# Order of plain and dilated heads, and the place of the rank matmuls, in a fused attention and expert kernel

## The chip, the cores and the metric

The kernel runs on one core of a Trainium2 chip. Its time is the device time of one execution in microseconds (us), as the median of several runs. The profile is of one further execution, with the hardware profiler on. Engines are named as in its page: PE is TensorE's matmuls, PEld its weight loads, DVE is VectorE, ACT is ScalarE, POOL is GpSimd and SP is SyncE; a "q" behind a name is the engine's sequencer, which also issues DMAs.

## The reference

Attention over 8 sequences of 576 tokens with 8 heads of 64, then one expert layer over the 4608 tokens (model width 512, 8 experts, hidden width 1024), each token going to one expert. Everything is float32.

```python
rel = pos[:, None] - pos[None, :]
mask_plain = (rel >= 0) & (rel < 32)                       # heads 0 to 3
mask_dil = (rel >= 0) & (rel < 32 * 4) & (rel % 4 == 0)    # heads 4 to 7
attn = softmax(where(mask, q @ k.T / 8, -1e9))
x = (attn @ v).transpose(0, 2, 1, 3).reshape(4608, 512)
logits = x @ w_gate
expert = argmax(logits, 1); gate = softmax(logits)[expert]
out = gate * (maximum(x @ w1[expert], 0) @ w2[expert])
```

## The kernel before

**Attention.** A head sees only a band, so scores are computed in blocks of 64 queries by 96 keys, nine blocks a head. For dilated heads the tokens are first put in order of their remainder by 4, which makes four strips of 144 tokens in which the mask is the same band. A *unit* is two heads of one kind in one sequence: `units` (line 472) lists `(b, ty, hl)`, 32 in all, with `ty` 0 for plain and 1 for dilated heads, and before the change plain comes first. Of a unit, `turn` transposes q and k on TensorE (lines 323 and 330) and copies them out of PSUM (VectorE for q, line 314, ScalarE for k, line 316). `front` makes the scores (line 366) and their row minima on VectorE (line 382); for sequences 0 to 3 (`EARLY`) the mask is added by matmuls (line 354), for later ones on VectorE. `exponentials` runs on ScalarE (line 403), `norm` on VectorE and GpSimd (lines 415 to 418), `weights` transposes the result (line 428) and VectorE copies it out (`eT`, line 430), `summed` multiplies by v (line 443). A unit's weights are made two units behind its scores (`LAG`), its sums three behind.

**Loads.** `load_qk` and `load_v` issue the DMAs from SyncE's queue; only k of sequence 0 goes by ScalarE's queue. A plain q or k of a sequence is 4 DMAs, one a head, in runs of 256 bytes (line 262). A dilated one is 4 DMAs, one for each of the four pieces of its strips, all four heads together, in runs of 512 bytes (line 269). v is 5 DMAs for plain heads and 13 for dilated ones. Each of these tiles has one buffer, so the load for the next sequence waits until the engines have read the last one, and SyncE's queue is in order. The mask tiles come by GpSimd's queue (`load_masks`): the first holds `turn` and `even0`, for plain heads, the second `even1` and `odd1`, for dilated ones.

**Routing.** `row_part` transposes the attention's output into token rows and `logit_part` makes the gate's logits (line 560), adding up over the four units of a sequence. When the last unit of a sequence has given its logits, `route(b)` starts: transpose of the logits (`lg`, line 577), one-hot vectors of the best expert and running counts on VectorE (lines 597 to 618, `before` being the counts), then two matmuls into `rank` (lines 625 and 632) that give each token its place in its expert, then the places as integers and six indirect DMAs from GpSimd that scatter the rows into a `bucket` in HBM (line 234). `tables` then works out, in small VectorE instructions, which expert's rows each *slot* of 128 tokens takes.

**Expert layer.** `moe` goes through some 37 slots. Of a slot, x is fetched from the bucket (line 1075), transposed (line 1150), multiplied by w1 (line 1218), then by w2 (line 1250), scaled and scattered to the output (line 1267). Weights are fetched by SyncE (line 1094).

**What sets the order.** The whole kernel is written as three generators that yield pieces: attention, routing and slots. A loop at the end takes one piece of attention (five a unit), then enough pieces of slots to keep a planned rate, and then one piece of routing. `yield` in `route` is thus what puts distance between two steps of routing. A finished table lets its slots start `BEHIND` = 12 planner's us later. After the last piece of attention, each piece of routing is given 2 us of slots:

```python
    while routing:
        clock["owed"] = 2.0
        run_slots()
        run_routing()
```

Within this, the scheduler of the language places instructions in each engine's in-order queue. All matmul outputs but the logits share one pool of seven PSUM banks (`bank`). `tc.issue_after(i)` makes what is issued in it stand behind instruction i on its engine.

Of the kernel before, what the change touches and what calls it, by code (L numbers as in the profile page):

```python
# [79 lines left out]
def _constants():  # L80


    def band(j, ty):

        qi, ki = 64 * j + np.arange(64)[:, None], max(0, 64 * j - WIN) + np.arange(96)[None]
        seen = (qi - ki >= 0) & (qi - ki < WIN)
        if ty:
            seen &= qi // STRIP == ki // STRIP
        return np.where(seen, 0.0, BIG)

    def mask(ty):

        pairs = [(0, 1), (2, 3), (4, 5), (6, 7), (8, 8)]
        return np.concatenate([np.concatenate([band(j, ty) for j in two]) for two in pairs], 1)

    p = np.arange(128)
    e = np.arange(E)

    parts = {"add0": mask(0)[:, 0:384], "add1": mask(1)}
    for name, ty, js in (
        ("even0", 0, (0, 2, 4, 6, 8, 8)), ("even1", 1, (0, 2, 4, 6, 8)), ("odd1", 1, (1, 3, 5, 7, 8))
    ):
        parts[name] = np.tile(np.concatenate([band(j, ty) for j in js], 1), (2, 1))
    parts["turn"] = np.tile(np.eye(64), (2, 1))

    exact, mask_at = [], {}
    for names in (("turn", "even0"), ("even1", "odd1"), ("add0", "add1")):
        n = 0  # L110
        for name in names:
            mask_at[name] = len(exact), n
            n += parts[name].shape[1]
        some = np.concatenate([parts[name] for name in names], 1).astype(np.float32)
        exact.append(np.ascontiguousarray(some.astype(ml_dtypes.bfloat16)))
    mask_at["odd0"] = mask_at["even0"][0], mask_at["even0"][1] + 96
    parts = {
        "tri": np.triu(np.ones((128, 128)), 1)[:, :96],
        "ones": np.ones((128, 128)),
        "rev": np.tile(E - e, (128, 1)),  # L120
        "ecap": np.tile(e * CAP, (128, 1)),
        "tok": p[:, None] + TT * np.arange(NT)[None],
        "row": p[:, None],
        "eidx": np.tile(np.minimum(np.arange(E1), E - 1), (128, 1)),
        "twice": np.tile(2 * np.arange(NSLOT), (128, 1)),
    }
    parts["first"] = np.tile(np.append(np.arange(E)[::-1] / E, -1e6), (128, 1))


    for s, (_, j0, j1) in enumerate(STAGES[:-1]):  # L130
        k = np.arange(j1 - j0)
        n = (j1 - j0 + 1) // 2
        parts[f"list{s}"] = np.tile(k // 2 + n * (k % 2), (128, 1))


    k, i, m = np.arange(NSLOT - J0), np.arange(NMIX), np.arange(NMIX + 1)
    n = k[:, None] - (np.array(MIX)[None] < k[:, None]).astype(int) @ (i[:, None] < m[None])
    last = {}
    last["plan"] = np.concatenate([n // 2, n % 2]).reshape(1, -1)
    last["many"] = m  # L140
    last["i2"] = i
    last["ends"] = -1 - i
    own = [[G * (g if g < n else g - n) for g in range(4)] for n in KIND]
    last["own"] = (np.array(own).reshape(1, -1))
    last["later"] = (G * np.array(KIND))
    at, k, cols = {}, 0, []
    for name, a in parts.items():
        full = np.zeros((128, a.shape[1]), np.float32)
        full[: a.shape[0]] = a
        at[name] = (k, a.shape[1])  # L150
        k += a.shape[1]
        cols.append(full)
    last_at, k = {}, 0
    for name, a in last.items():
        last_at[name] = (k, a.size)
        k += a.size
    last = np.concatenate([a.reshape(1, -1) for a in last.values()], 1).astype(np.float32)
    return np.ascontiguousarray(np.concatenate(cols, 1)), at, exact, mask_at, np.ascontiguousarray(last), last_at
# [3 lines left out]
def kernel(  # L162
# [46 lines left out]
    def const(name, rows=128):  # L209
        a, w = at[name]  # L210
        return cst[0:rows, a : a + w]
# [40 lines left out]

    t = {}

    def load_qk(b, ty):
        for name, src, queue in (("q", q, nc.sync), ("k", k, nc.sync if b else nc.scalar)):
            if ty == 0:
                x = pool.tile([TT, NT, 4, DH], F32, tag=name + "0", name=f"{name}0_{b}", bufs=1)  # L260
                for h in range(4):
                    queue.dma_start(x[:, :, h, :], src[b, h].rearrange("(t p) d -> p t d", p=TT))
            else:


                x = pool.tile([96, 4, 3, 128], F32, tag=name + "1", name=f"{name}1_{b}", bufs=1)
                a = src[b, 4:8].rearrange("h (t m a) d -> m t h (a d)", m=2, a=2)
                for i, p0, m, t0, n in ((0, 0, 0, 0, 96), (1, 0, 0, 96, 48), (1, 48, 1, 0, 48), (2, 0, 1, 48, 96)):
                    queue.dma_start(x[p0 : p0 + n, :, i], a[m, t0 : t0 + n])
            t[b, name, ty] = x  # L270

    def first_key(j):
# [32 lines left out]
    def turn(b, ty, hl, name):  # L305

        src = t[b, name, ty]

        def copy(out, in_):

            if name == "q":
                nc.vector.tensor_scalar(out, in_, -SCALE, None, op0=OP.mult)  # L314
            else:
                nc.scalar.copy(out, in_)  # L316

        dst = pool.tile([128, S], F32, tag=name + "T", name=name + "T", bufs=2)
        for a in range(2):
            ps = bank("turned")  # L320
            if ty == 0:
                for i in range(3):
                    nc.tensor.transpose(  # L323
                        ps[:, TT * i : TT * i + TT],
                        src[:, 3 * a + i, 2 * hl : 2 * hl + 2, :].rearrange("p h d -> p (h d)"),
                        ident[0:TT, 0:TT],
                    )
            else:
                for i in range(3):
                    nc.tensor.transpose(  # L330
                        ps[:, 96 * i : 96 * i + 96], src[:, 2 * hl + a, i], ident[0:96, 0:96]
                    )
            copy(dst[:, 288 * a : 288 * a + 288], ps[:, 0:288])
        return dst
# [134 lines left out]
    def attention():  # L469


        units = [(b, ty, hl) for b in range(B) for ty in range(2) for hl in range(2)]
        load_masks(0)
        for ty in range(2):
            load_qk(0, ty)
        load_masks(1)
        for ty in range(2):
            load_v(0, ty)

        wrote_bucket(nc.sync.dma_start(bucket[E * CAP : NROWS], blank), 0)  # L480
        qT = {n: turn(0, 0, 0, n) for n in "qk"}
        evs, dens, eTs, xTs = {}, {}, {}, {}
        for i in range(len(units) + LAG + 3):

# [23 lines left out]
            if 0 <= u - 1 < len(units):  # L508
                b2, ty2, hl2 = units[u - 1]
                logit_part(b2, 2 * ty2 + hl2, xTs.pop(u - 1))  # L510
                ended = b2 if (ty2, hl2) == (1, 1) else None
            yield 3.0, ended

            if 0 <= i - LAG < len(units):
# [19 lines left out]

    def row_part(b, c, xT):

        if c == 0:
            rows[b] = pool.tile([TT, NT, ROW], F32, tag="rows", name=f"rows_{b}")
            logits[b] = lpsum.tile([96, 2 * TT], F32, tag="logits", name=f"logits_{b}")
            nc.gpsimd.tensor_scalar(  # L540
                rows[b][:, :, DM + 1], const("tok", TT), float(b * S), None, op0=OP.add
            )
        for i in range(0, NT, 3):
            ps = bank("xrow")
            for n in range(3):
                nc.tensor.transpose(
                    ps[0:TT, 128 * n : 128 * n + 128],
                    xT[:, TT * (i + n) : TT * (i + n) + TT],
                    ident,
                )  # L550
            (nc.scalar.copy, nc.vector.tensor_copy)[i // 3](
                rows[b][:, i : i + 3, 128 * c : 128 * c + 128],
                ps[0:TT, 0:384].rearrange("p (t d) -> p t d", t=3),
            )

    def logit_part(b, c, xT):


        for j in range(3):
# [1 line left out]
                logits[b][32 * j : 32 * j + 32],  # L561
                lhsT=wg[:, c],
                rhs=xT[:, 2 * TT * j : 2 * TT * j + 2 * TT],
                start=c == 0,
                stop=c == 3,
            )

    def route(b):
# [47 lines left out]
        for i in range(NT):  # L616
# [1 line left out]
            nc.vector.tensor_tensor(  # L618
                out=before[:, n + 1], in0=before[:, n], in1=oh[:, i], op=OP.add
            )  # L620
        yield
        yield
        ps = bank("rank")
        rk = ps[0:TT, 0 : NT * E]
        nc.tensor.matmul(
            rk,
            lhsT=const("tri", TT),
            rhs=oh.rearrange("p t e -> p (t e)"),
            start=True,
            stop=False,  # L630
        )
        nc.tensor.matmul(
            rk,
            lhsT=const("ones", TT)[:, 0:TT],
# [27 lines left out]
    def tables(s):  # L662
# [5 lines left out]
        scratch = None  # L668
        if last:

            scratch = pool.tile([96, 4, 9, DH], F32, tag="v0", name="scratch", bufs=1)
            scratch = scratch.rearrange("p a b c -> p (a b c)")[0:1]
            width = packed_last.shape[1]
            nc.scalar.dma_start(
# [698 lines left out]
```

## Time and profile before

| | |
|---|---|
| time, median of 3 runs | 785.97 us (782.84 to 792.31) |
| time of the profiled execution | 786.18 us |
| its span in the profile | 784.4 us |
| granted TensorE clock, mean | 0.981 |
| PE busy | 744.8 us, 95% of the span |
| DVE, ACT, POOL busy | 279.7, 226.2, 146.2 us |
| DMA | 195.41 MB, 249 GB/s in the mean |
| first scores (L366) | 12.57 us |
| first slot's transposes (L1150) | 121.43 us |
| last tables of routing done | 524.7 us |
| last slot's w2 matmuls (L1250) begin | 764.60 us |

The span falls into a start until about 36 us, in which the first loads arrive, attention alone until 121 us, attention and slots together until the middle of the span, and slots alone after that. Starts and durations are in us from the span's start. In a timeline the number in brackets is how long the engine stood idle before, and what ended that. In a list of waits the numbers are the total, how often, and the longest. In windows, each engine has its busy time and its instructions, followed by the granted clock, the DMA engines' busy share and GB/s.

### The profile page before, as it was taken

What the parts mean: (1) busy time and instruction counts of PE and PEld (TensorE: products, weight loads), DVE (VectorE), ACT (ScalarE), POOL (GpSimd) and SP (SyncE); (2) the same over time, 40 slices, a digit from 0 to 9 for tenths busy, and PEclk for the clock granted to TensorE, in tenths of its full rate; (3) what the DMA queues carried; (4) which work ended last, traced back from release to release, by engine and by line L of the source; (5) the groups of instructions that cost most, each with busy time, mean ns of one, the idle gap of its engine ahead of it and who ended that gap; (6) DMA issues with size and microseconds to landing.
All of it is one profiled execution on the core that took longest, in us unless ns stands there. A gap on an engine that the chain in (4) does not pass through costs nothing. (4 is left out here: it accounts for less than half of the span.)

```text
span 784.4 us, 17928 instructions
## 1 busy us (share of the span) xinstructions
PE 744.8 (95%) x6774; PEld 555.8 (71%) x6774; DVE 279.7 (36%) x954; ACT 226.2 (29%) x853; POOL 146.2 (19%) x142
## 2 busy tenths in 40 slices
PE   5798898989999899999999999999999999999993
PEld 4686788778777677777777776786776383686781
DVE  3577779646334333353333421271010111111010
ACT  3696685533532233333322110100100100100100
POOL 0424334214112311122011300160000000000000
PEclk9899889999999999999999999999999999999997
DMA  9777589998998997999217827999980583983995
GB/s 202 191 146 207 143 214 302 298 255 254 314 300 274 353 321 225 313 333 342 74 53 246 285 94 279 320 340 390 330 302 32 201 307 133 327 288 130 325 316 206
DMA packets 179612, 195.41 MB, mean 249 GB/s; under 512 B 73552, under 2 KB 105952, under 8 KB 179522
## 3 DMA queue, kind: packets, MB, share of 16 engines
q1 hardware_dynamic: 166896, 169.01, 69.8%
q0 software_dynamic: 6928, 20.53, 7.4%
q10 hardware_dynamic: 5698, 4.67, 2.1%
q8 instruction: 57, 0.93, 0.5%
q14 instruction: 33, 0.27, 0.1%
HBM read 216.14 MB, written 21.54 MB: 303 GB/s over the span
## 5 line engine op out<-in xcount | busy, mean ns | idle before, releaser
L1218 PEld LDWEIGHTS ph<-xt,w 128*128 128x128 f32 x2240 | 259.9, 192 | 19.7 <-issue 16.9
L1218 PE MATMUL ph<-xt,w 128*128 128x128 f32 x2240 | 268.7, 276 | 3.1 <-DMA w<-in_moe_w_dram 2.1
L1250 PE MATMUL py<-w,h 128*128 128x512 f32 x560 | 255.2, 596 | 0.0
L1250 PEld LDWEIGHTS py<-w,h 128*128 128x128 f32 x560 | 100.2, 190 | 98.4 <-issue 96.0
L1267 POOL DMA_INDIRECT out_dram<-y,to x35 | 34.6, 988 | 322.6 <-ACT y L1261 306.1
L1152 DVE COPY xt<-xt 128x512 f32<-128x512 f32 x38 | 26.2, 690 | 184.7 <-PE xt L1150 184.5
L1261 ACT ACTIVATE y<-py,x 128x512 f32<-128x512 f32 x35 | 24.0, 687 | 217.2 <-PE py L1250 166.7
L418 POOL TENSOR_TENSOR e<-e,rec 128x864 f32<-128x864 f32 x32 | 52.2, 1631 | 173.1 <-DVE rec L417 104.3
L430 DVE COPY eT<-weights 96x384 f32<-96x384 f32 x96 | 47.7, 545 | 31.5 <-PE weights L428 31.2
L234 POOL DMA_INDIRECT bucket<-rows,idx x48 | 44.5, 927 | 72.4 <-DVE idx L651 60.2
L403 ACT ACTIVATE e<-e,lo 128x96 f32<-128x96 f32 x144 | 51.8, 361 | 13.7 <-DVE lo L395 13.7
L403 ACT ACTIVATE e<-scores,lo 128x96 f32<-128x96 f32 (+1 forms) x160 | 52.7, 345 | 4.5 <-DVE lo L382 4.1
L1238 DVE TENSOR_SCALAR h<-ph 128x512 f32<-128x512 f32 x35 | 24.1, 689 | 73.4 <-PE ph L1218 73.3
L1229 ACT ACTIVATE h<-ph 128x512 f32<-128x512 f32 x35 | 20.9, 597 | 86.3 <-PE ph L1218 82.4
L443 PEld LDWEIGHTS xo<-eT,v 96*64 96x64 f32 x1216 | 40.6, 145 | 6.4 <-issue 2.0
L443 PE MATMUL xo<-eT,v 96*64 96x64 f32 (+1 forms) x1216 | 44.9, 231 | 0.2 <-ACT kT L316 0.2
L316 ACT COPY kT<-turned 128x288 f32<-128x288 f32 x64 | 22.6, 406 | 58.7 <-PE turned L330 34.9
L428 PE MATMUL weights<-ident,e 128*96 128x128 f32 x288 | 38.8, 282 | 0.8 <-POOL e L418 0.8
L428 PEld LDWEIGHTS weights<-ident,e 128*96 128x96 f32 x288 | 32.8, 131 | 9.0 <-issue 7.6
L366 PE MATMUL scores<-kT,qT 64*64 64x96 f32 x1152 | 37.0, 258 | 0.0
L366 PEld LDWEIGHTS scores<-kT,qT 64*64 64x64 f32 x1152 | 31.7, 141 | 6.7 <-issue 3.8
L314 DVE TENSOR_SCALAR qT<-turned 128x288 f32<-128x288 f32 x64 | 26.3, 447 | 28.0 <-PE turned L323 16.1
(213 smaller groups left out, 589.2 us busy)
## 6 DMA issues: line engine op xcount, KB each, us to landing
w<-in_moe_w_dram SPq DMA_DIRECT2D x164, 1024.0 KB
x<-bucket SPq DMA_DIRECT2D x26, 257.0 KB
v<-in_v_dram SPq DMA_DIRECT2D x32, 192.0 KB
q<-in_q_dram SPq DMA_DIRECT2D x32, 144.0 KB
v<-in_v_dram SPq DMA_DIRECT2D x48, 96.0 KB
k<-in_k_dram SPq DMA_DIRECT2D x28, 144.0 KB
q<-in_q_dram SPq DMA_DIRECT2D x16, 192.0 KB
x<-bucket ACTq DMA_DIRECT2D x11, 257.0 KB
```

The source lines that it names most:

```text
L234: nc.gpsimd.indirect_dma_start(out=bucket, out_offset=bass.IndirectOffsetOnAxis(ap=idx, axis=0), in_=rows, in_offset=None, bounds_check=NR ...
L314: nc.vector.tensor_scalar(out, in_, -SCALE, None, op0=OP.mult)
L366: nc.tensor.matmul(sc[r][64 * c : 64 * c + 64, 96 * (i % 5) : 96 * (i % 5) + 96], lhsT=qT[rows, 64 * j : 64 * j + 64], rhs=kT[rows, first_ ...
L403: nc.scalar.activation(out=e[p0:p1, i], in_=s[:, 96 * (i - i0) : 96 * (i - i0) + 96], func=AF.Exp, bias=lo[p0:p1, i : i + 1], scale=-1.0, ...
L418: return nc.gpsimd.tensor_tensor(out=e, in0=e, in1=rec.unsqueeze(2).broadcast_to([128, 9, 96]), op=OP.mult)
L428: nc.tensor.transpose(tp[0:96, 128 * i : 128 * i + 128], e[:, a + i], ident)
L430: nc.vector.tensor_copy(eT, tp[0:96, 0:384])
L443: nc.tensor.matmul(xo[DH * h : DH * h + DH, at0 : at0 + nq], lhsT=vt[:, 2 * hl + r, j, :] if ty == 0 else vt[:, hl, j, DH * r : DH * r + D ...
L1152: nc.vector.tensor_copy(xt, ps)
L1218: nc.tensor.matmul(ph[:, fi], lhsT=w1[:, c, 128 * f : 128 * f + 128], rhs=xt[:, c], start=c == 0, stop=c == 3,)
L1250: nc.tensor.matmul(py, lhsT=h[:, f], rhs=w2[:, f], start=f == 0, stop=f == 7)
L1267: i = nc.gpsimd.indirect_dma_start(out=out, out_offset=bass.IndirectOffsetOnAxis(ap=to, axis=0), in_=y, in_offset=None, bounds_check=N - 1 ...
```

## The change

Units run dilated heads first in each sequence, and everything that names the first or last unit of a sequence follows (the start and end of the logits' sum, when the row tile is made, when a sequence has ended). Loads follow the same order. The mask tiles are grouped anew, so that the first holds what dilated heads need. For sequence 0 alone, dilated q and k are loaded in eight DMAs each, the four pieces for the first two heads and then for the other two. `route` yields five times, not twice, between the running counts and the rank matmuls, and the first rank matmul is tied behind the last q or k transpose traced by then (`turns[-1]`). The scratch of the last tables takes the buffer of dilated v.

```diff
-    for names in (("turn", "even0"), ("even1", "odd1"), ("add0", "add1")):
+    for names in (("turn", "even1", "odd1"), ("even0",), ("add0", "add1")):
...
-    t = {}
+    t, turns = {}, []
+
+
+    STRIPS = ((0, 0, 0, 0, 96), (1, 0, 0, 96, 48), (1, 48, 1, 0, 48), (2, 0, 1, 48, 96))
...
-                for i, p0, m, t0, n in ((0, 0, 0, 0, 96), (1, 0, 0, 96, 48), (1, 48, 1, 0, 48), (2, 0, 1, 48, 96)):
-                    queue.dma_start(x[p0 : p0 + n, :, i], a[m, t0 : t0 + n])
+                for i, p0, m, t0, n in STRIPS:
+                    if b:
+                        queue.dma_start(x[p0 : p0 + n, :, i], a[m, t0 : t0 + n])
+
+                for hl in () if b else range(2):
+                    h = slice(2 * hl, 2 * hl + 2)
+                    for i, p0, m, t0, n in STRIPS:
+                        queue.dma_start(x[p0 : p0 + n, h, i], a[m, t0 : t0 + n, h])
...
-                    nc.tensor.transpose(
-                        ps[:, 96 * i : 96 * i + 96], src[:, 2 * hl + a, i], ident[0:96, 0:96]
+                    turns.append(
+                        nc.tensor.transpose(
+                            ps[:, 96 * i : 96 * i + 96], src[:, 2 * hl + a, i], ident[0:96, 0:96]
+                        )
                     )
...
-        units = [(b, ty, hl) for b in range(B) for ty in range(2) for hl in range(2)]
+        units = [(b, ty, hl) for b in range(B) for ty in (1, 0) for hl in range(2)]
         load_masks(0)
-        for ty in range(2):
+        for ty in (1, 0):
             load_qk(0, ty)
         load_masks(1)
-        for ty in range(2):
+        for ty in (1, 0):
             load_v(0, ty)
...
-        qT = {n: turn(0, 0, 0, n) for n in "qk"}
+        qT = {n: turn(0, 1, 0, n) for n in "qk"}
...
-                ended = b2 if (ty2, hl2) == (1, 1) else None
+                ended = b2 if (ty2, hl2) == (0, 1) else None
...
-        if c == 0:
+        if c == 2:
...
-                start=c == 0,
-                stop=c == 3,
+                start=c == 2,
+                stop=c == 1,
...
-        yield
-        yield
+
+        for _ in range(5):
+            yield
         ps = bank("rank")
         rk = ps[0:TT, 0 : NT * E]
-        nc.tensor.matmul(
-            rk,
-            lhsT=const("tri", TT),
-            rhs=oh.rearrange("p t e -> p (t e)"),
-            start=True,
-            stop=False,
-        )
+        with tc.issue_after(turns[-1].ins):
+            nc.tensor.matmul(
+                rk,
+                lhsT=const("tri", TT),
+                rhs=oh.rearrange("p t e -> p (t e)"),
+                start=True,
+                stop=False,
+            )
...
-            scratch = pool.tile([96, 4, 9, DH], F32, tag="v0", name="scratch", bufs=1)
+            scratch = pool.tile([96, 2, 9, 2 * DH], F32, tag="v1", name="scratch", bufs=1)
```

More of the change, by code (lines that the diff above doesn't have):

```diff
@@ L322, in turn @@
                 for i in range(3):
[L323 to L326, printed above, removed]
+                    turns.append(
+                        nc.tensor.transpose(
+                            ps[:, TT * i : TT * i + TT],
+                            src[:, 3 * a + i, 2 * hl : 2 * hl + 2, :].rearrange("p h d -> p (h d)"),
+                            ident[0:TT, 0:TT],
+                        )
                     )
@@ L329, in turn @@
                 for i in range(3):
-                    nc.tensor.transpose(
-                        ps[:, 96 * i : 96 * i + 96], src[:, 2 * hl + a, i], ident[0:96, 0:96]
+                    turns.append(
+                        nc.tensor.transpose(
+                            ps[:, 96 * i : 96 * i + 96], src[:, 2 * hl + a, i], ident[0:96, 0:96]
+                        )
                     )
@@ L620, in route @@
             )
-        yield
-        yield
+        for _ in range(5):
+            yield
         ps = bank("rank")
         rk = ps[0:TT, 0 : NT * E]
-        nc.tensor.matmul(
-            rk,
-            lhsT=const("tri", TT),
-            rhs=oh.rearrange("p t e -> p (t e)"),
-            start=True,
-            stop=False,
-        )
+        with tc.issue_after(turns[-1].ins):
[5 more added lines that the diff above has]
+                stop=False,
+            )
         nc.tensor.matmul(
```

## Prediction, made before the changed kernel ran

> **What bounds the kernel now.** I read the share of busy time first: TensorE is busy 95% of the span and its row of tenths is 9 nearly everywhere from slice 3 on, so time is won only where TensorE stands still or runs slowly. Then I asked who TensorE waits for. In the first 120 us (columns: waiter and releaser, us in total, times, longest):
>
> ```profile
> PE turned L323 <- DMA q<-in_q_dram: 7.6, 3, 6.1
> PE rank L632 <- DVE before L618: 3.0, 2, 1.5
> PE turned L323 <- DMA k<-in_k_dram: 2.2, 2, 1.6
> PE rank L625 <- DVE gate L639: 1.5, 1, 1.5
> PE rank L625 <- ACT dl L612: 1.5, 1, 1.5
> ```
>
> Two causes: loads of q and k (start-up, and the first unit of sequence 1), and the two rank matmuls of routing, 6.0 us. After 120 us the whole list is 6.8 us:
>
> ```profile
> PE xt L1150 <- DMA x<-bucket: 2.7, 1, 2.7
> PE ph L1218 <- DMA w<-in_moe_w_dram: 2.1, 1, 2.1
> PE ph L1218 <- DVE xt L1152: 1.0, 1, 1.0
> PE rank L632 <- DVE before L618: 0.9, 1, 0.9
> ```
>
> The timeline of TensorE shows what a rank stall costs in all (start, us, instruction, idle time before it):
>
> ```profile
> 58.42 0.66 PE L323 MATMUL turned<-ident,q 96*128 96x96 f32 x6
> ...
> 62.34 0.34 PE L625 MATMUL rank<-oh,cst 96*96 96x48 f32 x2 [1.48 <-ACT dl L612]
> ...
> 64.72 0.37 PE L632 MATMUL rank<-before,cst 96*96 96x48 f32 x2 [1.55 <-DVE before L618]
> ...
> 65.82 2.17 PE L443 MATMUL xo<-eT,v 96*64 96x64 f32 x36
> ...
> 69.60 0.66 PE L323 MATMUL turned<-ident,q 96*128 96x96 f32 x6
> ```
>
> From one q turn to the next is a unit of attention: 11.18 us here. Undisturbed it is 6.22 to 6.55 (starts 45.72, 52.20, 58.42 and 75.26, 81.81, 88.04). The same 36 xo matmuls that take 2.17 us here took 1.27 at 55.57. The windows name the reason, the granted clock (the column behind POOL):
>
> ```profile
> 66.00:68.00 2.00, 2.00 (x37) 1.88 (x36) 1.36 (x5) 0.76 (x3) 1.40 (x2) 0.50 0.15 40
> 96.00:98.00 2.00, 2.00 (x40) 1.78 (x36) 1.44 (x4) 0.33 (x2) 1.61 (x2) 0.50 0.20 51
> ```
>
> Each pair of stalls leaves TensorE at half clock for some us. In VectorE's timeline the releaser is:
>
> ```profile
> 62.38 1.62 DVE L640 TENSOR_SCALAR gate<-gate 96x6 f32<-96x6 f32 x1
> 63.92 0.15 DVE L618 TENSOR_TENSOR before<-before,oh 96x8 f32<-96x8 f32 x1
> 64.04 0.19 DVE L641 RECIPROCAL rows<-gate 96x6 f32<-96x6 f32 x1
> 64.15 0.71 DVE L618 TENSOR_TENSOR before<-before,oh 96x8 f32<-96x8 f32 x4
> ```
>
> Six elements take 1.62 us (median of that line 0.168) while GpSimd's L418 runs, 62.35 to 63.98. VectorE is late, not short of time.
>
> **What the Trainium skill says.** "TensorE: Matmul & The Clock Gate", Part 1: the array's clock falls to half after about one idle window of 3.4 us and returns after a busy one. The trace agrees on the half clock (0.50), though two gaps of 1.5 us with 0.8 us of work between were enough. "GPSIMD Engine Reference", Key points: GpSimd shares SBUF interfaces with VectorE and contends with 2-port or two-input instructions; L640's 1.62 us beside L418's 1.63 fits. "DMA: Bandwidth & Descriptors", Specifications: runs below 512 B miss line rate. Plain heads load in 256 B runs, dilated in 512 B; the page of before shows no stretch with one kind alone under equal load. The same page, Issuing engines are not separate DMA queues: moving loads between queues saves only issue time.
>
> **The change part by part.**
>
> *Rank matmuls.* In the changed order of TensorE, between sequence 0's lg and its rank stand a full unit of attention and a q turn (turns, xrow, scores, xo, logits, weights): some 7 us of matmuls, where L618 ended 6.4 us after lg. So TensorE no longer waits on rank. Worth, sequence 0: 11.18 - 6.2 (a unit) - 0.5 (the rank matmuls) = 4.5, of it 3.0 idle and 1.5 clock. Sequence 1: q turns at 88.04 and 100.78, so 12.74 - 6.2 - 0.6 (rank, tot) = 5.9, and the next unit takes 6.95 (to 107.73), 0.75 over, since the clock is 0.50 to beyond 102: 6.7. Sequence 2: 0.95. Later sequences wait for nothing. Sum: 4.5 + 6.7 = 11.2, and 0.95.
>
> *What is late next.* On VectorE the chain stays ahead of the same unit's minimum L382. Before, L382 began at 65.92; it cannot begin before L618 ends, 64.86. TensorE, no longer stopped, would have those scores by about 62.0, and L382 normally follows by 0.6: VectorE is 2.3 us late. Behind it stand the copies of eT and qT that free the seven buffers of the pool of PSUM banks: two of scores, three of weights and two of a q turn fill them, so the k turn waits for eT. Bounds: nothing (slack of a lag of two units) to 2.3 us per sequence. I take 1.5 in sequences 0 and 1, since in an undisturbed unit the eT copy runs right behind the weights: 3.0 back. One stall of 1.5 should not halve the clock. For sequence 2, expert matmuls lie between: half of 0.95 is won. Net 11.2 - 3.0 + 0.5 = **8.7 us won**.
>
> *Routing three pieces later.* Scatters on GpSimd (six, 0.92 to 1.0 us each), tables on VectorE and the fetches of x and w on SyncE all come that much later, and the first slot about one unit later in TensorE's order. Work is only moved: TensorE is saturated in attention alone too (16.17 of 16.45 us busy from 41.80). Cost 0; without that cover see the third rival. At the end, three more pieces with 2 us of slots each put the last tables from 524.7 to 531; the last slot starts at 757.02 and slots are 14.45 apart, so slot 24, the first that needs them, comes about 584. Cost 0.
>
> *Order of heads.* Same matmuls and bytes. Start-up: ScalarE issues twelve k loads, not eight, ahead of its first kT copy (12.11), at 0.54 each 2.2 us, but the last issues of before already waited for landings (four took 5.58 us), and the same 1.18 MB must land first. I take 0; bounds -1 (longer runs) to +2.2. Sequence 1's first unit: before, its k turn needed two heads' DMAs of four and began at 32.60 after a 1.63 us wait; dilated loads of later sequences are not split, so all four strips are needed, 0.29 MB more, at the 225 GB/s of 32 to 34 us 1.3 us. SyncE has four more loads ahead of them, 2.1 us at 0.53, under the landings. I take **1.3 lost**; bounds -1 to +3.
>
> *The x wait.* Slot 2's x was issued at 163.77, behind eight q/k loads that held SyncE from 147.78; in the changed order it stands behind v of plain heads and ahead of q and k. The 2.7 us may go or come back elsewhere (0 to 2.7, or 3 lost): I take half, **1.4 won**. Masks in other groups, turns kept in a list, and scratch in v1's buffer, free by then: 0, GpSimd's same two mask issues covering it.
>
> **Sum**: 8.7 - 1.3 + 1.4 = 8.8. The profiled execution took 786.18 (span 784.4 and 1.8 around), 0.2 above the median of 785.97: 786.18 - 8.8 = 777.4, on the median's scale **777 us**. A measurement tells about 2% from no change (the runs of before differ by 1.2%), so this counts as within 2%.
>
> **Rivals.**
> 1. *VectorE returns nothing and the x wait goes*: 11.2 + 0.95 + 2.7 - 1.3 = 13.6: 772.5. For: attention alone keeps VectorE at 71% (11.71 of 16.45). Against: the routing chain adds some 5 us with the 1.5 of contention to one unit of 6.2.
> 2. *The wait changes its place*: TensorE stops for banks or for ScalarE (14.55 of 16.45 busy) by 3.5 per sequence and part of the clock loss stays: 11.2 - 7.0 - 1.3 = 3: 783. For: L382 gains only 1.06 us. Against: TensorE has a lag of two units.
> 3. *Slower: x arrives late.* Routing is three of five pieces later; in the shared stretch a unit takes 10 to 20 us (scores at 136.07, 146.09, 156.82, 177.27), so 6 to 12 later. If the slots do not move as far, the first slot of each of five stages waits for x: at 4 us each 20, less 8.7: 797. It outweighs the gain above 1.8 us per stage. Against: the planner releases slots a fixed distance behind the tables.
>
> **Numbers.** Forecast case (773 to 781) 0.52; rival 1 (770 to 773) 0.17, and below 770, with start-up too, 0.06; rival 2 (781 to 785) 0.16; rival 3 0.08; 0.01 for the rest. The range 770 to 784 leaves out the tail below, rival 3 and the end of rival 2. Faster by over 2% (below 770.3): 0.09; slower by over 2% (above 801.7): 0.03.
>
> **What would show it.** Right: no rank line in TensorE's waits, clock 1.00 from 58 to 105, q turns 6.2 to 8 us apart around sequence 0's lg, first xt still near 121 though a unit later in the order (121.4 + 6.2 - 8.2 + 1.3 = 120.7). Rival 2: a wait of turned or scores on DVE eT, DVE lo or ACT e of over 2 us there. Rival 3: xt waits for x at each stage. The head's step: the k turn of sequence 1's first unit at 34, not 32.6. Wrong would be a start-up later by more than 3 us.

## The result, and the profile after

The changed kernel takes 793.88 us in the median of 16 runs (787.87 to 796.78), the kernel before 786.00 in 16 runs (782.84 to 792.31). The ratio is 1.0088, with a 95% interval of [1.0064, 1.0112]: within 2%, but on the other side of no change than the 777 us that were forecast. The profiled execution took 790.71 us, its span is 788.8 us against 784.4, so the trace shows +4.4 of the +7.9. The granted clock is 0.982 in it; the runs between 794 and 797 us had 0.972 to 0.977, and of those no trace is kept, so the other 3.5 us have no trace that explains them. The experiments below were measured in five later series, each with the kernel before in it: it takes 787.75 us in one of them and 842.5 to 846.0 us in the other four, and whether the chip or something else makes that difference is not known.

The waits of TensorE after, first 120 us (columns: waiter and releaser, us in total, times, longest):

```profile
PE turned L342 <- DMA q<-in_q_dram: 6.8, 5, 3.3
PE turned L342 <- ACT xT L477: 3.9, 2, 1.9
PE weights L441 <- POOL e L431: 3.5, 4, 1.2
```

And the whole list after 120 us:

```profile
PE ph L1234 <- DVE xt L1168: 5.5, 1, 5.5
PE logits L574 <- ACT xT L477: 1.1, 2, 0.8
PE scores L379 <- ACT kT L325: 0.5, 1, 0.5
```

The rank lines are gone, as are the waits for x and w. In their place q turns wait for ScalarE's `xT`, and the first slot waits 5.5 us for its own copy on VectorE, where it waited 1.0. In all, TensorE's stops with a named releaser are 25.9 us before and 25.7 after: they moved and did not grow.

I follow the first scores of the units, counted from 0. Unit 7 is the last of sequence 1; the rank rounds of sequences 0 and 1 lie between units 7 and 13.

| | before | after | late_plain (below) |
|---|---|---|---|
| unit 7, first scores | 54.45 | 57.84 | 52.06 |
| unit 13, first scores | 104.00 | 104.88 | 92.54 |
| units 7 to 13 | 49.55 | 47.04 | 40.48 |
| first slot's w1 matmuls | 123.62 | 136.44 | 121.83 |
| span | 784.4 | 788.8 | 781.0 |

So the changed kernel loses 3.4 us by unit 7, wins 2.5 in the two rank rounds, and loses 3.5 from there to the end.

**Where the rank stop went.** TensorE's timeline around sequence 0's rank matmuls, after (start, us, instruction, idle time before it):

```profile
61.73 0.33 PE L591 MATMUL lg<-ident,lgs 96*96 96x96 f32 x2
...
68.18 0.41 PE L342 MATMUL turned<-ident,q 96*128 96x96 f32 x3
70.54 0.47 PE L342 MATMUL turned<-ident,q 96*128 96x96 f32 x3 [1.95 <-ACT xT L477]
70.84 0.29 PE L641 MATMUL rank<-oh,cst 96*96 96x48 f32 x2
...
73.91 1.60 PE L379 MATMUL scores<-kT,qT 64*64 64x96 f32 x36
```

The rank matmuls run without a wait, but the q turn in front of them stops halfway for 1.95 us. VectorE's and then ScalarE's timeline tell why:

```profile
66.09 1.62 DVE L656 TENSOR_SCALAR gate<-gate 96x6 f32<-96x6 f32 x1
67.63 0.15 DVE L632 TENSOR_TENSOR before<-before,oh 96x8 f32<-96x8 f32 x1
67.75 0.19 DVE L657 RECIPROCAL rows<-gate 96x6 f32<-96x6 f32 x1
67.85 0.52 DVE L632 TENSOR_TENSOR before<-before,oh 96x8 f32<-96x8 f32 x3
68.29 0.55 DVE L395 TENSOR_REDUCE lo<-scores 128x4 f32<-128x384 f32 x1
```

```profile
69.17 0.34 ACT L416 ACTIVATE e<-scores,lo 128x96 f32<-128x96 f32 x1 [2.24 <-DVE lo L395]
...
69.82 0.66 ACT L477 COPY xT<-xo 128x288 f32<-128x288 f32 x1
```

TensorE finished these scores at 65.48. Their minima begin at 68.29, since the routing chain stands ahead of them, one instruction of it stretched to 1.62 us beside GpSimd's multiply (L431, from 66.05, 1.64 us). ScalarE waits 2.24 us for the minima, and behind its exponentials, in the same in-order queue, stands the copy of `xo` that frees a PSUM bank. TensorE needs that bank for the second half of the q turn. The rank matmuls have no part in this chain; a bank comes free late. The granted clock falls some us later, as it did before the change (columns as in the windows of before, the granted clock behind POOL):

```profile
66.00:70.00 4.00, 2.59 (x46) 2.06 (x42) 3.89 (x14) 1.53 (x6) 1.64 (x1) 1.00 0.33 85
70.00:74.00 4.00, 3.39 (x27) 2.79 (x31) 2.69 (x8) 3.98 (x20) 0.00 (x0) 0.71 0.35 93
```

In sequence 1 the same q turn stops for 1.94 us, until 100.70, and half clock follows again (0.50 from 103 to 105).

**The start.** TensorE around the q and k turns of sequence 1's first unit, after:

```profile
31.05 0.39 PE L342 MATMUL turned<-ident,q 96*128 96x96 f32 x1 [1.45 <-DMA q<-in_q_dram]
32.94 0.39 PE L342 MATMUL turned<-ident,q 96*128 96x96 f32 x1 [1.50 <-DMA q<-in_q_dram]
33.61 0.90 PE L342 MATMUL turned<-ident,q 96*128 96x96 f32 x4 [0.28 <-DMA q<-in_q_dram]
...
35.23 0.58 PE L342 MATMUL turned<-ident,k 96*128 96x96 f32 x2
...
38.28 0.39 PE L342 MATMUL turned<-ident,k 96*128 96x96 f32 x2
...
39.53 0.39 PE L342 MATMUL turned<-ident,k 96*128 96x96 f32 x2
...
40.46 1.04 PE L379 MATMUL scores<-kT,qT 64*64 64x96 f32 x36
```

Before:

```profile
32.60 1.20 PE L323 MATMUL turned<-ident,k 96*128 96x96 f32 x6 [1.63 <-DMA k<-in_k_dram]
...
35.33 1.89 PE L366 MATMUL scores<-kT,qT 64*64 64x96 f32 x36
```

The q turn waits strip by strip, three times, 3.2 us in all (the other two of its five waits, 3.6 us, are unit 0's), and the k turn comes in three pieces with other matmuls between them. The unit's scores begin at 40.46 and no longer at 35.33. Little of this shows in the list of waits: TensorE's waits for q and k fall from 9.8 us to 8.2. It shows in the busy time. Up to unit 7's first scores, before and then after:

```profile
0.00:54.45 54.45, 41.04 (x620) 33.90 (x621) 28.29 (x84) 34.27 (x164) 13.52 (x17) 0.94 0.90 185
0.00:57.84 57.84, 45.59 (x620) 34.39 (x621) 29.82 (x84) 34.43 (x164) 13.53 (x17) 0.94 0.80 176
```

As many matmuls, 620, keep TensorE busy for 4.6 us longer at the same mean clock, and it stands idle 1.2 us less. Of the 4.6, the turns have 2.8 (13.52 and 16.29 us for the same 96): at full clock a pair of them takes 0.39 us, as at 38.28, and six in a row take 0.66, as in the prediction's timeline. The ends of matmuls are modelled in the profile, so busy times are approximate.

**The first slot**, TensorE's timeline and then VectorE's, after:

```profile
130.27 0.66 PE L1166 MATMUL xt<-ident,x 128*128 128x128 f32 x4
136.44 2.07 PE L1234 MATMUL ph<-xt,w 128*128 128x128 f32 x8 [5.51 <-DVE xt L1168]
```

```profile
135.24 0.17 DVE L428 TENSOR_SCALAR den<-den 128x9 f32<-128x9 f32 x1 [3.45 <-ACT e L416]
135.44 0.22 DVE L430 RECIPROCAL rec<-den 128x9 f32<-128x9 f32 x1
135.69 0.69 DVE L1168 COPY xt<-xt 128x512 f32<-128x512 f32 x1
```

The first slot now comes when sequence 4 has begun, the first whose mask VectorE adds. The copy of its transposed x stands in VectorE's queue behind `den` of that unit, and `den` waits for all nine exponentials. Before, the same copy stood behind a `den` that waited 0.46 us:

```profile
122.69 0.17 DVE L415 TENSOR_SCALAR den<-den 128x9 f32<-128x9 f32 x1 [0.46 <-ACT e L403]
...
122.89 0.68 DVE L1152 COPY xt<-xt 128x512 f32<-128x512 f32 x1
```

The stop after the change is followed by half clock until 139.92:

```profile
136.44:139.92 3.48, 3.48 (x16) 3.40 (x17) 0.64 (x2) 0.00 (x0) 1.02 (x1) 0.50 1.05 202
```

### The profile page after: what moved, and what is told of

Its sections match the earlier page's. It is cut to its first block, busy times and chain, and to the rows that moved or that the text cites. A ratio compares the mean times of both kernels' runs of the same rounds, so it can differ in the third digit from the quotient of the medians.

```text
span 788.8 us, 17958 instructions
## 1 busy us (share of the span) xinstructions
PE 749.8 (95%) x6774; PEld 555.2 (70%) x6774; DVE 286.8 (36%) x954; ACT 225.7 (29%) x853; POOL 146.5 (19%) x142
## 4 chain that ended last, share of the span: by engine, by line
PE 82%; ACT 6%; DVE 4%; issue 2%; DMA 2%; another core or an unknown queue 1%; SPq 0%; POOLq 0%; POOL 0%; ACTq 0%; DVEq 0%
PE ph L1234 31%; PE py L1266 29%; ACT e L416 4%; PE xo L456 3%; PE scores L379 3%; PE weights L441 2%; PE xrow L560 2%; PE xt L1166 2%; PE ph L1196 2%; PE py L1196 2%; PE turned L342 2%; PE logits L574 1%; PE turned L333 1%; DMA k<-in_k_dram 1%
## 5 line engine op out<-in xcount | busy, mean ns | idle before, releaser
L431 POOL TENSOR_TENSOR e<-e,rec 128x864 f32<-128x864 f32 x32 | 52.3, 1634 | 140.1 <-DVE rec L430 113.3
L416 ACT ACTIVATE e<-e,lo 128x96 f32<-128x96 f32 x144 | 51.8, 361 | 16.7 <-DVE lo L408 16.7
L456 PE MATMUL xo<-eT,v 96*64 96x64 f32 (+1 forms) x1216 | 42.9, 224 | 0.2 <-ACT kT L325 0.2
L456 PEld LDWEIGHTS xo<-eT,v 96*64 96x64 f32 x1216 | 38.5, 138 | 4.6 <-ACT kT L325 0.5
L441 PEld LDWEIGHTS weights<-ident,e 128*96 128x96 f32 x288 | 32.1, 129 | 12.4 <-issue 7.6
```

Source lines behind the costliest of these rows:

```text
L416: nc.scalar.activation(out=e[p0:p1, i], in_=s[:, 96 * (i - i0) : 96 * (i - i0) + 96], func=AF.Exp, bias=lo[p0:p1, i : i + 1], scale=-1.0, ...
L431: return nc.gpsimd.tensor_tensor(out=e, in0=e, in1=rec.unsqueeze(2).broadcast_to([128, 9, 96]), op=OP.mult)
L441: nc.tensor.transpose(tp[0:96, 128 * i : 128 * i + 128], e[:, a + i], ident)
L456: nc.tensor.matmul(xo[DH * h : DH * h + DH, at0 : at0 + nq], lhsT=vt[:, 2 * hl + r, j, :] if ty == 0 else vt[:, hl, j, DH * r : DH * r + D ...
```

## The experiments

Ratios are to the kernel before in the same series. At the level of 842 to 846 us engines stop for up to 20 us with no releaser that the profile names ("remote" in its lists), in the kernel before too; a difference of a few us between kernels there may be such stops falling elsewhere. A further run of a kernel in another series has a number behind its name.

### The two halves alone

`rank_only` is the kernel before with

```diff
-        yield
-        yield
+
+        for _ in range(5):
+            yield
         ps = bank("rank")
         rk = ps[0:TT, 0 : NT * E]
-        nc.tensor.matmul(
...
+        with tc.issue_after(turns[-1].ins):
+            nc.tensor.matmul(
...
```

`heads_only` is the changed kernel with this undone: two yields and no tie. `before_2` is the kernel before itself, run for its trace.

> The kernel before with the rank matmuls five pieces behind the one-hots and tied behind a q or k transpose; plain heads still first. Theory A (VectorE's chain stands ahead of the next unit's row minima, so the wait only moves to a PSUM bank that ScalarE frees late; and the first slot, one unit later, waits for its xt copy behind the denominators): no rank line in TensorE's waits, instead turned waits about 2 us for ACT xT in sequences 0 and 1, and ph waits 4 to 6 us for the first xt copy; start-up as before; 785 to 790 us. Theory B (all that was lost comes from the order of heads and its loads): 4 to 8 us faster than before, 778 to 782 us.

> The changed kernel with the two pieces of before and no tie ahead of the rank matmuls, so that the order of heads, its loads and its masks alone are changed. Theory A: the start-up loses about 3.5 us (unit 7's scores at 58 instead of 54.5 us, since all strips of sequence 1 must land), rank waits of 6 us stay, no wait of ph for the first xt: 788 to 791 us. Theory B: most of what was lost, 792 to 795 us. A theory in which the order of heads costs nothing: 786 us.

> The rank half of the change alone, plain heads first as before. Theory A (each cause a TensorE stop of its own, sizes from the changed kernel's trace: start 3.4 lost by the head order, rank rounds 1.3 won, first slot 5.5 and some 2.4 of half clock lost, x, w and small waits up to 6.8 won): the changed kernel's ratio less 3.4 us of start, so 1.000 to 1.006, with a wait of the q turns for ACT xT in sequences 0 and 1 and one of 5 to 7 us of the first slot for its copy. Rival (the two halves don't add, each alone costs the whole): 1.007 to 1.011.

> The order of heads alone, two pieces and no tie as before. Theory A: start 3.4 to 6 us lost, the rank stops as before (6 us), first slot's wait under 2; ratio 1.003 to 1.008. If the loss of the whole change comes from the later rank alone: 0.998 to 1.002.

> The kernel before itself, for its trace on this chip. On a chip of the usual kind 784 to 788 us, units' first scores as in the first trace within 1 us. On one of the unusual kind about 842 us with stops without a named cause of the same places and lengths as in the changed kernels there.

> The rank half alone. Theory A (each stop counts once, sizes from the changed kernel's trace): changed kernel less 3.4 us of start: ratio 1.000 to 1.006, with q turns that wait for ACT xT in sequences 0 and 1 and a first slot that waits 5 to 7 us for its copy. Rival (each half alone costs the whole): 1.007 to 1.011.

> The order of heads alone. Theory A: 3.4 to 6 us lost at the start, rank stops as before, first slot's wait under 2: ratio 1.003 to 1.008. Rival: 1.007 to 1.012; if the loss of the whole comes from the later rank alone: 0.998 to 1.002.

> The rank half alone. On a chip where the kernel before takes 784 to 790 us: theory A (each stop counts once) ratio 0.997 to 1.005; rival (each half alone costs the whole) 1.007 to 1.011. On one where it takes 840 us or more: 1.008 again, and nothing new.

> The order of heads alone. On a chip where the kernel before takes 784 to 790 us: theory A 1.003 to 1.008; rival, that the loss of the whole comes from the rank half alone, 0.998 to 1.002. On one where it takes 840 us or more: 1.008 to 1.011 again.

All four series were at the level of 842 to 846 us, so only ratios can be held against the expectations in us.

| | 1 | 2 | 3 | 4 |
|---|---|---|---|---|
| before, us | 842.71 | 842.54 | 846.02 | 842.90 |
| rank_only, ratio | 1.0087 | 1.0097 | 1.0081 | 1.0097 |
| heads_only, ratio | 1.0092 | 1.0115 | 1.0074 | 1.0098 |

Each interval lies above 1 (the lowest is [1.0035, 1.0113], heads_only_3). At this level each half alone costs 0.7 to 1.2%, which is what the rival said and more than the trace's stops explained. The traces of one series, before_2 beside the two halves, show part of how. From the lists of waits, all engines in before_2, and TensorE in rank_only_3:

```profile
ACT xT L457 <- remote: 30.8, 4, 10.9
```

```profile
PE ph L1224 <- DVE xt L1158: 7.2, 1, 7.2
...
PE py L1256 <- DVE h L1244: 13.0, 1, 13.0
...
PE turned L324 <- ACT xT L461: 2.8, 2, 1.4
```

ScalarE stands still for 10.9 us ahead of two `xT` copies in the kernel before (and for 20.0 ahead of one `h`), and VectorE for 12.4 of TensorE's 13.0 in rank_only_3, where "remote" is all that the trace names. The last line shows what theory A said: with plain heads first, too, the rank lines go and the q turn stops for `xT`, 1.4 us in each of sequences 0 and 1; all four traces of rank_only have it, and the 7.2 us of the first slot. heads_only_3 is behind before_2 by 8.3 us at unit 7 and by 5.6 at the last output: there the half's loss is its start. rank_only_3 is 0.6 us behind at unit 7, has no rank stop, is 9.3 us ahead at unit 13, then waits 7.2 for its first slot's copy, and is 5.5 behind at the last output. The 13.0 don't explain that: the slot with that stop takes 29.4 us (from 567.4), and before_2 has a slot of 29.7 (from 546.3) of its own. So for the order of heads the place is shown; for the later rank, the first slot's stop is, and the rest of its loss at this level isn't placed. At the level of 787 us neither half alone was measured.

### Running counts behind the minima, and the first slot earlier

`late_adds` is the changed kernel with

```diff
-        for i in range(NT):
-            n = b * NT + i
...
-        for _ in range(5):
+        for _ in range(3):
+            yield
+        with tc.issue_after(minima[-1].ins):
+            for i in range(NT):
+                n = b * NT + i
+                nc.vector.tensor_tensor(
+                    out=before[:, n + 1], in0=before[:, n], in1=oh[:, i], op=OP.add
+                )
+            nc.vector.tensor_reduce(out=gate, in_=dl, axis=AX, op=OP.add)
+            nc.vector.tensor_scalar(gate, gate, 1e-9, None, op0=OP.add)
+            nc.vector.reciprocal(row[:, :, DM], gate)
+
+        for _ in range(2):
             yield
...
-        nc.vector.tensor_reduce(out=gate, in_=dl, axis=AX, op=OP.add)
-        nc.vector.tensor_scalar(gate, gate, 1e-9, None, op0=OP.add)
-        nc.vector.reciprocal(row[:, :, DM], gate)
```

where `minima` lists the instructions of lines 395 and 408. `behind9` is the changed kernel with `BEHIND` 9 in place of 12, which puts the first slot's copy on VectorE ahead of the mask, the minima and `den` of that unit.

> The changed kernel with the running counts and the gate's three instructions on VectorE traced three pieces later and tied behind the next unit's row minima, still ahead of the rank matmuls. Theory A: the two waits of turned for ACT xT (1.95 and 1.94 us) and the half clock behind them go, lg to lg is 25 to 27 us instead of 30.2 and 30.6; the first slot's 5.5 us stay: 785 to 789 us. Rival (the bank is late because ScalarE itself is short of time, not because the minima are late): the waits stay within 0.5 us, 792 to 795 us.

> The changed kernel with the planner's distance between finished tables and their slots cut from 12 to 9, which puts the first slot's transposes and its copy on VectorE ahead of the row minima and denominators of that round. Theory A: the 5.5 us wait of ph for the first xt goes, the rest stays: 787 to 790 us. Rival (the wait is VectorE's backlog at that time and turns up elsewhere in the same round): 792 to 795 us.

> The changed kernel with the running counts and the gate behind the next unit's row minima. Theory A: the stops for ACT xT in sequences 0 and 1 go and units 7 to 13 gain 6 to 8 us on the changed kernel; the start and the first slot's copy stay; late_plain's 0.991 plus 3.4 to 5 us: ratio 0.995 to 0.999. Rival (late_plain is fast through its plain order, not through its counts): 1.004 to 1.010.

late_adds gave 1.0088 [1.0066, 1.0109] and 1.0084 [1.0065, 1.0103], behind9 1.0081 [1.0059, 1.0103], all at the level of 842 us, where the changed kernel itself was not run. These are the rivals' ratios. The stops named in the expectations did shrink: no dilated q turn (line 342) waits for `xT` in the two traces of late_adds, though a plain one (line 333) does at about 116 us, for 2.1 and 2.4 us, and the first slot's wait is 4.3 us there and 3.5 in behind9. In behind9 the first slot's copy is ahead of the masks, and stands behind a routing chain in place of them. That no gain shows in the ratios kept the question open, and it was put again on plain heads, in one series at the level of 787 us.

### Plain heads first, counts behind the minima

`late_plain` is rank_only with the edit of late_adds; `late_plain_b9` adds `BEHIND` 9; `late_split_b9` is that with dilated heads first and sequence 1's loads split; `split1` is the changed kernel with only that split:

```diff
-                    if b:
+                    if b > 1:
...
-                for hl in () if b else range(2):
+                for hl in () if b > 1 else range(2):
```

> Plain heads first as in the kernel before, rank matmuls tied five pieces on, and of those five three stand ahead of the running counts and the gate, which are traced behind the next unit's row minima on VectorE. Theory A (order of heads, VectorE's chain and the first slot's copy each cost TensorE a stop of their own, and add up): no stop for ACT xT and no start-up loss; the first slot's copy still stands behind den of the first unit that VectorE masks, so its wait of 4 to 5.5 stays; against the kernel before ratio 0.998 to 1.004. Theory B (the loss is a lower clock or slower instruction supply that goes with any later routing): ratio 1.007 to 1.012 as for the other kernels with late rank matmuls.

> The same with BEHIND 9 in place of 12, by which the first slot's copy on VectorE stands ahead of that unit's masks and den. Theory A: the wait of the first slot's transposes falls from about 5 to under 3 us and the time by as much: ratio 0.993 to 1.000, under late_plain by 3 to 5 us. Theory B: as late_plain, 1.007 to 1.012.

> The same with dilated heads first, and sequence 1's dilated q and k in eight DMAs each, two heads at a time, as in sequence 0. Theory A: as late_plain_b9 but for the start of the first units, lost 0 to 2 us by the split loads: ratio 0.995 to 1.002. If dilated heads cost their 3.4 us whatever the split: late_plain_b9 plus 3.4. Theory B: 1.007 to 1.012.

> The changed kernel with sequence 1's dilated q and k in eight DMAs each, two heads at a time. Theory A, that the q turns of sequence 1's first unit wait for the strips of all four heads: their waits on q (6.8 us in all) fall by 2 us or more, unit 7 starts by 56.5 and not 57.8, and the time is 1 to 2 us under the changed kernel's. Rival, that the loads as a whole are late (the bytes ahead of them, not the shape of the DMAs): unit 7 stays at 57.5 to 58.5, and the time is the changed kernel's within 1 us.

| before 787.75 us | us | ratio, 95% interval |
|---|---|---|
| late_plain | 781.97 | 0.9913 [0.9879, 0.9947] |
| late_plain_b9 | 785.79 | 0.9971 [0.9945, 0.9998] |
| late_split_b9 | 785.47 | 0.9965 [0.9947, 0.9983] |
| split1 | 789.57 | 1.0030 [1.0009, 1.0050] |

late_plain is faster than the kernel before by 0.9%, in four runs, and below the range of both theories, so a later rank does not have to cost time: the theory that it always does (B in the expectations) falls. The changed kernel was not in this series; its own ratio is 1.0088. late_plain's VectorE and then TensorE timeline at sequence 0's rank matmuls:

```profile
59.77 1.45 DVE L386 TENSOR_REDUCE lo<-scores 128x4 f32<-128x384 f32 x4
61.25 0.36 DVE L625 TENSOR_TENSOR before<-before,oh 96x8 f32<-96x8 f32 x1
...
61.77 0.17 DVE L629 TENSOR_SCALAR gate<-gate 96x6 f32<-96x6 f32 x1
```

```profile
62.00 0.66 PE L324 MATMUL turned<-ident,q 96*128 96x96 f32 x6
62.85 0.37 PE L637 MATMUL rank<-oh,cst 96*96 96x48 f32 x2 [0.19 <-DVE eT L434]
```

The minima run first, the gate takes 0.17 and not 1.62 us, and the 1.95 us stop is gone. Units 7 to 13 take 40.5 us, 9.1 less than before, at a clock of 1.00. This edit moves the order and takes the contention away at once; which of the two weighs more was not tried.

Of 11.5 us ahead at unit 13 only 3.4 are left in the span. The first slot of late_plain still waits 5.0 us for its copy, and begins its w1 matmuls just 1.8 us ahead of the kernel before. Taking the copy out from behind `den` doesn't help. TensorE's waits in late_plain_b9, first part and after 130 us:

```profile
PE ph L1227 <- DMA w<-in_moe_w_dram: 4.0, 1, 4.0
...
PE xt L1159 <- DMA x<-bucket: 7.3, 1, 7.3
```

The weights are next, at 118.2 us, and a later slot's x costs 7.3 where late_plain waits 3.5: late_plain_b9 is 3.8 us slower in the median. The expectation of a further 3 to 5 us won was wrong.

late_split_b9 is late_plain_b9 with dilated heads first, and it is as fast (785.47 and 785.79 us), as its theory A said. With sequence 1's loads split, the order of heads thus costs nothing that this series can tell.

### The loads split, and late_plain in another series

`late_split` is late_adds with the split of split1; `late_plain_2` is late_plain again.

> The same and sequence 1's dilated q and k in eight DMAs each, BEHIND 12. Theory A: 1 to 4 us under late_adds_2, as late_plain: ratio 0.990 to 0.995. Rival (dilated heads first cost time beside the loads too): as late_adds_2, 0.995 to 0.999.

> Plain heads first, rank tied, running counts behind the minima. On a chip where the kernel before takes 784 to 790 us: 0.988 to 0.995, as late_plain. On one where it takes 840 us or more: theory A, that the head order's 5 to 7 us is what late_split (1.005) still loses there: 0.996 to 1.001; rival, that later routing loses there whatever is mended: 1.004 to 1.008.

late_split gave 1.0048 [1.0029, 1.0068], outside both ranges; it takes 3.4 us less than late_adds_2 of the same series (847.06 against 850.44). late_plain_2 gave 1.0021 [1.0007, 1.0034], between the two ranges; it takes 6.0 us less than rank_only_4 of the same series (844.44 against 850.47). Both series were at the level of 842 us, where late_plain thus does not beat the kernel before, though counts behind the minima still win over rank_only. All traces together show the start, as first scores of unit 4, sequence 1's first, at both levels:

| order and loads | traces | unit 4, us | unit 7, us |
|---|---|---|---|
| plain first | 9 | 34.1 to 35.7 | 51.8 to 54.4 |
| dilated first | 8 | 40.3 to 42.2 | 57.7 to 62.1 |
| dilated first, sequence 1 split | 3 | 34.9 to 37.8 | 52.2 to 56.1 |

The first two groups lie 4.6 us or more apart at unit 4, so the order of heads costs that much there; the split loads lie between and reach into the first, so the shape of sequence 1's loads is about half of it or more. split1 met its theory A at unit 7 (56.15, expected by 56.5), not in the waits on q, which fell by 1.5 us where 2 were expected. In its trace the end does not follow, though: it reaches unit 13 3.3 us ahead of the changed kernel's trace, stops for 1.4, 0.6 and 0.55 us behind it, and stands level at sequence 2's `lg` (122.49 against 122.46). Its median is some 4 us under the changed kernel's all the same, in another series; this was not cleared up.

## Why the prediction was wrong, by its own steps

- **Rank matmuls.** Right: no rank line is left in TensorE's waits. 11.2 us was about the right size of what the stops cost: late_plain, which takes them away with no new one over 1.4 us, wins 9.1 between units 7 and 13.
- **What is late next.** This step failed most. It saw that the chain stands ahead of the minimum and puts it 2.3 us late, and took 1.5 a sequence, 3.0 back, through `eT` and the k turn. The changed kernel won 2.5 and not 8.2, so 8.7 of 11.2 came back. Held against late_plain, 6.6 us are missing between units 7 and 13. Of them, 3.9 are the stops of 1.95 and 1.94 through ScalarE's queue and the bank of `xo`, which the step did not follow, and some 3 (an estimate: half of the time that TensorE is busy at 0.50) are the half clock, which it excluded for one stall of 1.5. Two units of lag did not cover it. Rival 2 is what happened: its 3.5 per sequence and remaining clock loss were about the size, though its sign named other releasers (`eT`, `lo`, `e`) and over 2 us.
- **Routing three pieces later, cost 0.** The second failure. The step looked at rates, not at what the first slot's copy stands behind once the slot comes a unit later: 5.5 us of stop, and half clock behind it in 3.48 us of work, another 1.7. The first transposes came at 130.27 and not at 120.7. Moving the copy ahead by `BEHIND` brings out w and x, so not all of the 5.5 was to be had.
- **Order of heads.** The place was right, q and k of sequence 1 in whole strips, and the size too small: 1.3 with a bound of 3, measured 3.4 at unit 7 in the changed kernel and 3.2 or more between any trace with dilated heads first in whole strips and any with plain heads first. It was reckoned as one wait for bytes, 0.29 MB at 225 GB/s, with the k turn at 34. The turns come in pieces as the strips land, the k turn from 35.23 to 39.92, and TensorE loses the time in longer busy time, not in longer waits. Half clock has no part in the difference: it lasts 6.8 us there in both kernels. Unit 0 came no later (12.2 against 12.6). The prediction's own sign of being wrong, a start-up later by more than 3 us, is met at unit 7.
- **The x wait.** Half of 2.7 was taken; all of it went, and w's 2.1 too. They were won, and are in the +4.4.
- **Sum.** In the traces: rank 2.5 won where 8.2 were forecast; head 3.4 lost, not 1.3; the first slot 5.5 and 1.7 lost, not 0; x, w and the small waits before (1.0, 0.95) 6.7 won, not the 1.4 and 0.5 of the forecast; new small waits after unit 13 about 2.6 lost. This gives +4.0 for the +4.4 of the traces; the other 3.5 of the +7.9 in the medians stay open. The range 770 to 784 left rival 2 at its mild end and had no case in which the first slot stops. Rival 3 had the slower sign, but x arrives in time and its mechanism did not happen.

"TensorE: Matmul & The Clock Gate", Part 1 of the Trainium skill speaks of an idle window of 3.4 us ahead of the half clock. The trace differs: a single stop of 1.95 us was followed by a clock of 0.71 over the next 4 us, and the measurement decides. Nor does the length of a stop decide alone, so what the clock costs here can't be read from the stops' lengths. A stop of 2.69 us before the change, until 166.43, and split1's of 1.94 us, until 68.83, left the clock at 1.00; split1's of 1.95 us, until 81.72, was followed by 0.50. The kernel before, then split1 twice:

```profile
166.00:170.00 4.00, 3.57 (x32) 3.57 (x33) 1.46 (x3) 0.00 (x0) 0.67 (x1) 1.00 0.74 203
```

```profile
69.00:72.00 3.00, 2.93 (x57) 2.51 (x56) 2.33 (x8) 2.98 (x16) 0.00 (x0) 1.00 0.37 96
82.00:85.00 3.00, 3.00 (x19) 2.94 (x18) 2.34 (x5) 0.40 (x3) 0.00 (x0) 0.50 1.17 195
```

Two other places of the skill that the prediction names, on runs of 256 and 512 bytes and on the queues that issue loads, are put to the test by no run here.

## What to carry to other kernels

When a wait of the bounding engine is taken away, follow the same queue one instruction further: the small chain that made TensorE wait for ranks also stood ahead of the row minima, and through ScalarE's order it held a PSUM bank. Moving the waiting instruction helps little until the chain itself is moved behind the work that others need. The three kernels here that beat the kernel before, late_plain, late_plain_b9 and late_split_b9, all have that, in the series at 787 us; late_plain alone was measured at the other level, and does not beat it there. For a stage that starts later, look up which instructions its first copies will stand behind, and for a load that is to come earlier, how many landings the first reader needs, not only how many bytes; what that costs may stand in the busy time and not in the waits.

## What had not been expected

- late_plain is worth 0.991 at the level of 787 us and 1.002 at that of 842, where engines stop without a named releaser. The cause was not tried.
- A clock that stays low for some us after one stop of about 2 us, in some places and not in others: behind sequence 0's stop the score matmuls took 1.60 us in place of 1.03 to 1.2.
